# Both masks and both diagonals of a unit in one slot each, the second expert product two column tiles behind, and the first step's weight splits, states and chunks in the order of the first block's needs

## The chip, the cores and the metric

The kernel runs on one core of one Trainium2 chip. The time is device microseconds (us) of one execution. A kernel has one figure, the median of several runs. One execution is also taken by the profiler, and the rows in this document come from it.

Five queues run side by side, each in its own order: TensorE (PE, with its weight loads as PEld), VectorE (DVE), ScalarE (ACT), GpSimd (POOL) and the queue that issues transfers (SP). An instruction starts when the one ahead of it in its queue lets it and when the semaphores that it waits for are set.

## The reference

The computation is a linear attention with decay, followed by two gated expert layers. The sizes are: batch 4, 8 heads, 768 positions, head width 48.

```python
for t in range(S):                       # S = 768
    cur = np.einsum('bhd,bhe->bhde', u[None] * kt, vt)
    y[:, :, t] = np.einsum('bhd,bhde->bhe', rt, state + cur)
    state = w[None, :, :, None] * state + np.einsum('bhd,bhe->bhde', kt, vt)
x = y.transpose(0, 2, 1, 3).reshape(B * S, H * D)        # 3072 x 384
m = ((x @ w_a) * (x @ w_b)) @ w_out                      # width 1536
return (((m @ w1) * (m @ w2)) @ w3) @ w_out2             # width 1024
```

## The kernel before, in words

**Attention in chunks.** The 768 positions are cut into 6 chunks of 128. A chunk of one batch element is a unit, numbered 0 to 23 with the batch element running fastest, so units 0 to 3 are chunk 0 and units 4 to 7 chunk 1. A unit makes scores on PE (L363), takes the part below the diagonal with a mask on DVE (`a_evac`, L374, one instruction for each half of the heads), writes the diagonal into it (`a_diag`, L380, again one for each half), multiplies by the values (`y_mm`: L399 with the state, then L403 with the scores), and updates the state (`s_mm` L464, `s_decay` L471, `s_upd` L481). `prep_r`, `prep_k` and `prep_d` prepare the next unit's inputs, mostly on POOL; `k_nat` scales k there (L356). Units 0 to 3 have their own code ahead of everything else, because they have no state yet.

**Expert products.** A step is one chunk of all four batch elements, 512 columns. For each of 12 column tiles f, `ab_slots` makes two products on PE (two blocks of nine matmuls, L616). ACT copies the first to `g` (L635), DVE multiplies (L641), ACT rounds the product to `gh` (L642) and DVE makes the remainder `gl` (L647). `m_mm` then multiplies `gh` and `gl` by w_out in nine matmuls (L667 to L669) into three accumulators. Each operand is a high and a low part, which is why there are three matmuls for each product.

**Weight splits.** The weights arrive as 8-byte words. Class `Stream` turns each piece of 128x512 (a job) into a high and a low part: three DVE instructions convert the bits (L96, L112, L115, where L96 is that of the next job), ACT rounds the high part (`cast`, L128, followed by two range tests L131 and L150), and DVE subtracts to get the low part (L148). The first layer has 27 jobs: three for each of six groups of w_a and w_b columns (`wab0` to `wab5`, each used by two column tiles), and three for each of three groups of w_out rows (`wo0` to `wo2`, each used by four column tiles).

**What sets the order.** The order of the program text is the order in every queue; there is no scheduler. `merge` puts it together for each step: the main slots (products and `m_mm`), with the slots of the next chunk's units spread between them, and in the first step the remaining splits (`late`: `step` finishes a job and converts the next, `st.cast` rounds it) spread between these. A product's slot forces the splits that it needs. The prologue (the loop over u at L580) makes some splits itself: the tables `STEPS_U`, `STEPS_K` and `TAIL` say how many.

Of the kernel before, what the change touches and what calls it, by code (L numbers as in the profile page):

```python
# [7 lines left out]
F32 = mybir.dt.float32  # L8
# [12 lines left out]
C = 128  # L21
# [16 lines left out]

WARM, WARM_0 = 10, 6


STEPS_U = (1, 0, 0, 0)
STEPS_K = (0, 1, 1, 1)
TAIL = (1, 2)

S_NOW = 2
PRE = 3

END_0 = 4
LATE = 3  # L50
# [115 lines left out]
def rwkv_moe_kernel(ctx, tc, rkT, nat, wu, wab, wout, w12, w3T, wo2, r_in, k_in, v_in, w_in, u_in, out):  # L166
# [7 lines left out]
    def flat(ap):  # L174
        return ap.rearrange("p a b -> p (a b)")

    with tc.manual_schedule():
# [41 lines left out]
        wt, ut = wt[:, 0], wt[:, 1]  # L219
        load_rk(0)  # L220
        load_nat(0)
        u_bc = const.tile([128, DM], F32, name="u_bc")

        chk = const.tile([128, N64, 2], F32, name="chk")
        small = const.tile([128, 1], F32, name="small")
# [16 lines left out]
            for k in range(KD):  # L242
                wab_ready[i] = st.add(wab[i, :, k, :], lambda k=k: dst(k))

        def add_wout(i):
            def dst(s):
                if i not in wo_t:
                    wo_t[i] = [wop.tile([128, 4, DM], F32R, tag=f"wo{p}{i}", name=f"wo{p}{i}") for p in "hl"]
                return [flat(t)[:, s] for t in wo_t[i]]

            for j in range(3):
                s = slice(j * 512, (j + 1) * 512)
                wo_ready[i] = st.add(flat(wout[i])[:, s], lambda s=s: dst(s))

        def add_w12(i):
            w12_t[i] = [w12p.tile([128, KD, 512], F32R, name=f"w12{p}{i}") for p in "hl"]
            for k in range(KD):
                w12_ready[i] = st.add(w12[i, :, k, :], lambda k=k: [t[:, k, :] for t in w12_t[i]])

        for i in range(6):  # L260
            add_wab(i)
            if i % 2 == 0:
                add_wout(i // 2)
        st.AHEAD = 1
        for u in range(1, B):
            load_rk(u)
# [5 lines left out]
        def later_loads(u):  # L272
# [7 lines left out]
            elif u == 3:  # L280
# [5 lines left out]
        nc.gpsimd.memset(ident, 0.0)  # L286
        nc.gpsimd.affine_select(out=ident, in_=ident, compare_op=ALU.not_equal, fill=1.0,
                                base=0, pattern=[[-1, 128]], channel_multiplier=1)
        mask = const.tile([128, 128], F32, name="mask")
# [30 lines left out]
        tr = const.tile([112, NP, C], F32, name="tr")  # L320
        nc.vector.tensor_copy(out=tr[:, :, HALF:], in_=pos[:, :, 0:HALF])
        nc.vector.reciprocal(out=tr[:, :, 0:HALF], in_=pos[:, :, 1:][:, :, ::-1])
        tk = const.tile([112, NP, C], F32, name="tk")
# [127 lines left out]
        def s_mm(u):  # L451
            c, b = divmod(u, B)
            v = v_of(u)
            nat_t.pop(u, None)
            if c == NC - 1:
                return
            ps = (ps_at.tile([112, NP, D], F32, name="at") if c else
                  ps_m.tile([112, NP, D], F32, tag=("m2", "m0")[u % 2], name="s_ps"))
            at_ps["s", u] = ps
# [33 lines left out]
        def unit_slots(u):  # L493
            n = u + 1
            nxt = n < NU
            pool = nc.gpsimd

            def after(f, *a):
                if nxt:
                    f(n, *a)  # L500

            return [
                lambda: (scores(u), after(prep_r, pool)),
                lambda: (a_evac(u, 0), after(prep_k, pool)),
                lambda: (a_evac(u, 1), a_diag(u, 0), k_nat(u)),
                lambda: a_diag(u, 1),

                lambda: (y_mm(u), s_mm(u)),
                lambda: (load_rk(u + 2), load_nat(u + 2), y_evac(u), (u + 1) % B == 0 and y_shuffle(u // B), s_decay(u),
                         after(prep_d, 0)),  # L510
                lambda: (s_upd(u), after(prep_d, 1)),
                lambda: after(prep_d, 2),
            ]

# [46 lines left out]
            a_evac(u, 0)  # L561
            a_evac(u, 1)

        def steps(n):
            for _ in range(n):
                step()
                st.cast()

        prep_0(0)
        warm_up(WARM_0)  # L570
        scores_0(0)
# [8 lines left out]
        for u in range(B):  # L580
            if u + 1 < B:
                scores_0(u + 1)
                scores_d(u + 1)
            y_0(u)
            if u + 2 < B:
                prep_0(u + 2)
            if u + 1 < B:
                both_a(u + 1)
                diag_0(u + 1)
            y_0_evac(u)  # L590
            steps(STEPS_U[u])
            later_loads(u)
            if u == 2:
                tn_ps = ps_m.tile([128, NP, 112], F32, tag="m0", name="tn_ps")
                for p in range(NP):
                    mm(tn_ps[:, p, :], lhsT=tkw[:, p, :], rhs=ident[:112, :112], start=True, stop=True)
                tnat = const.tile([128, NP, 2, D], F32, name="tnat")
                for x, (a, e) in enumerate(XR):
                    nc.scalar.copy(out=tnat[:, :, x, :], in_=tn_ps[:, :, a:e])
            for b in ((), (), (0, 1), (2, 3))[u]:  # L600
                k_nat(b)
            steps(STEPS_K[u])
        steps(TAIL[0])
        for u in range(S_NOW):
            s_mm(u)
            s_upd(u)
        steps(TAIL[1])
        for f in prep_slots(B)[:PRE]:
            f()


        def ab_mm(ps, w, cs, x):
# [6 lines left out]
        def ab_slots(x, wget, keep):  # L619

            t = {}

            def run_a():
                w, ca, _ = wget()
                t["a"] = ps_ab.tile([128, TB], F32, name="ab")
                ab_mm(t["a"], w, ca, x())

            def run_b():
                w, _, cb = wget()
                t["b"] = ps_ab.tile([128, TB], F32, name="ab")  # L630
                ab_mm(t["b"], w, cb, x())

            def evac_a():
                t["g"] = gp.tile([128, TB], F32, tag="g", name="g")
                nc.scalar.copy(out=t["g"], in_=t["a"])  # L635

            def evac_b():
                g = t["g"]
                gh = gp.tile([128, TB], F32R, tag="gh", name="gh")
                gl = gp.tile([128, TB], F32R, tag="gl", name="gl")  # L640
# [16 lines left out]
        def m_mm(q, f):  # L657
            gh, gl = gt.pop((q, f))
            i, j = divmod(f, 4)
            if q == 0 and j == 0:  # L660
                st.split(wo_ready[i])
            if f == 0:
                m_ps[q] = [ps_m.tile([128, TB], F32, tag=f"m{k}", name=f"m{k}") for k in range(KD)]
            wh, wl = wo_t[i]
            for k in range(KD):
                cs = slice(k * 128, (k + 1) * 128)
                mm(m_ps[q][k], lhsT=wh[:, j, cs], rhs=gh, start=(f == 0), stop=False)  # L667
                mm(m_ps[q][k], lhsT=wh[:, j, cs], rhs=gl, start=False, stop=False)  # L668
                mm(m_ps[q][k], lhsT=wl[:, j, cs], rhs=gh, start=False, stop=(f == NF1 - 1))  # L669

        def m_evac(q):
            for k in range(KD):
                t = gp.tile([128, TB], F32, tag=("g", "gh", "gl")[k], name="m_sb")
                nc.scalar.copy(out=t, in_=m_ps[q][k])
                nc.sync.dma_start(out=m_d[q][:, k, :], in_=t)

# [46 lines left out]
        for q in range(NB):  # L723
            main = []
            for f in range(NF1):
                main += ab_slots(lambda q=q: xt[q], lambda q=q, f=f: w1_get(q, f),
                                 lambda *t, q=q, f=f: gt.__setitem__((q, f), t))
                lag.append((q, f))
                if len(lag) > 1:
                    main.append(m_slot(*lag.pop(0)))  # L730
            side = step_slots(q + 1)
            if q == 0:
                side = [lambda u=u: (s_mm(u), s_upd(u)) for u in range(S_NOW, B)] + prep_slots(B)[PRE:] + side
            if q == 0:
                late = [step, st.cast] * (len(st.jobs) - st.begun + 1)
                late += [lambda: None] * (len(late) // LATE)
# [359 lines left out]
```

## Time and profile before

| | |
|---|---|
| median of 3 runs | 926.12 us (925.85 to 927.89) |
| the profiled execution's own time | 927.42 us |
| its span, first to last instruction | 925.7 us |
| PE busy | 888.2 us, 96% |
| DVE busy | 447.2 us, 48% |
| ACT busy | 327.7 us, 35% |
| mean granted TensorE clock | 0.981 |

The span and the profiled execution's own time are of the same execution; 1.7 us lie outside the span. Busy shares are means over the whole span, and the kernel has stages with very different limits: the first 150 us and the rest have to be read apart.

### The profile page before, as it was taken

How to read it: one execution, taken by the hardware profiler on the slowest of the kernel's cores; microseconds unless marked ns; L12 is line 12 of the kernel's file. 1: busy time of each engine (PE TensorE's matmuls, PEld its weight loads, DVE VectorE, ACT ScalarE, POOL GpSimd, SP SyncE). 2: the span in 40 equal slices, each digit the busy share in tenths (PEclk: the TensorE clock that was granted, in tenths of full speed). 3: DMA queues.
4: the chain of work that ended last, by engine and by line, in shares of the span. 5: the costliest groups of instructions: out<-in, count | busy, mean ns of one | idle time of the engine just before them, and what ended most of it. 6: DMA issues, size and time to landing. Idle time of an engine off the chain costs nothing.

```text
span 925.7 us, 12522 instructions
## 1 busy us (share of the span) xinstructions
PE 888.2 (96%) x4962; PEld 753.1 (81%) x4962; DVE 447.2 (48%) x745; ACT 327.7 (35%) x737; POOL 122.0 (13%) x118
## 2 busy tenths in 40 slices
PE   8488879999999999999999999999999999999997
PEld 7366668888888888888888888899988888888886
DVE  8889894444334433443333789676332323222212
ACT  4375563322222223222121687655322212122211
POOL 2512322222222312320300000000000000000000
PEclk9789989999999999999999999999999999999999
DMA  8545432211222212222103345442020201010001
GB/s 250 180 142 170 145 114 63 80 46 59 65 66 64 78 47 71 66 64 64 62 2 106 127 146 189 143 146 95 12 69 0 69 1 57 12 35 1 35 0 38
DMA packets 26066, 73.57 MB, mean 79 GB/s; under 512 B 3152, under 2 KB 7376, under 8 KB 26000
## 3 DMA queue, kind: packets, MB, share of 16 engines
q1 hardware_dynamic: 26000, 72.70, 25.2%
q8 instruction: 41, 0.67, 0.3%
q14 instruction: 25, 0.20, 0.1%
HBM read 61.28 MB, written 9.44 MB: 76 GB/s over the span
## 4 chain that ended last, share of the span: by engine, by line
PE 86%; DVE 8%; ACT 2%; DMA 2%; issue 2%; SPq 0%; ACTq 0%
PE ab L616 50%; PE m L667 5%; PE m L668 5%; PE m L669 5%; PE at L764 4%; PE o L788 3%; PE o L789 3%; PE o L787 3%; PE at L403 2%; PE at L363 2%; DVE cvt L112 2%; DVE cvt L115 2%; PE at L399 2%; DVE cvt L96 1%; DMA rk<-in_rkT_dram 1%
## 5 line engine op out<-in xcount | busy, mean ns | idle before, releaser
L641 DVE TENSOR_TENSOR ab<-g,ab 128x512 f32<-128x512 f32 x120 | 83.4, 695 | 301.2 <-PE ab L616 299.8
L616 PE MATMUL ab<-xt,w12h 128*128 128x512 f32 x576 | 177.4, 389 | 0.0
L635 ACT COPY g<-ab 128x512 f32<-128x512 f32 x120 | 70.0, 583 | 250.5 <-PE ab L616 250.5
L642 ACT CAST gh<-ab 128x512 fp32r<-128x512 f32 x120 | 70.3, 586 | 239.4 <-DVE ab L641 239.4
L616 PEld LDWEIGHTS ab<-xt,w12h 128*128 128x128 f32 x576 | 107.5, 188 | 18.8
L647 DVE TENSOR_TENSOR gl<-ab,gh 128x512 fp32r<-128x512 f32 x120 | 82.8, 690 | 65.7 <-ACT gh L642 65.5
L616 PE MATMUL ab<-xt,w12l 128*128 128x512 f32 x288 | 112.0, 389 | 0.0
L668 PE MATMUL m<-gl,woh 128*128 128x512 f32 x216 | 84.9, 393 | 1.5 <-DVE gl L647 1.5
L667 PE MATMUL m<-gh,woh 128*128 128x512 f32 x216 | 86.2, 399 | 0.0
L669 PE MATMUL m<-gh,wol 128*128 128x512 f32 x216 | 84.5, 391 | 0.0
L336 POOL TENSOR_TENSOR rk<-rk,tr 112x512 f32<-112x512 f32 x20 | 27.4, 1368 | 293.1 <-DMA rk<-in_rkT_dram 249.0
L616 PEld LDWEIGHTS ab<-xt,w12l 128*128 128x128 f32 x288 | 54.1, 188 | 11.3
L616 PE MATMUL ab<-xt,wab0h 128*128 128x512 f32 x144 | 48.5, 420 | 4.2 <-ACT xt L427 4.2
L668 PEld LDWEIGHTS m<-gl,woh 128*128 128x128 f32 x216 | 40.8, 189 | 11.1 <-DVE gl L647 2.7
L667 PEld LDWEIGHTS m<-gh,woh 128*128 128x128 f32 x216 | 40.8, 189 | 9.9 <-issue 0.4
L669 PEld LDWEIGHTS m<-gh,wol 128*128 128x128 f32 x216 | 40.7, 188 | 8.6
L115 DVE SCALAR_TENSOR_TENSOR cvt<-stg_t,cvt 128x512 int32<-128x512 int32 x61 | 47.0, 770 | 0.3
L112 DVE SCALAR_TENSOR_TENSOR cvt<-stg_t,cvt 128x512 int32<-128x512 int32 x61 | 46.9, 770 | 0.3
L616 PE MATMUL ab<-xt,wab1h 128*128 128x512 f32 x144 | 46.6, 405 | 0.0
L616 PE MATMUL ab<-xt,wab2h 128*128 128x512 f32 x144 | 45.9, 400 | 0.0
L616 PE MATMUL ab<-xt,wab3h 128*128 128x512 f32 x144 | 45.4, 396 | 0.0
L616 PE MATMUL ab<-xt,wab4h 128*128 128x512 f32 x144 | 45.3, 396 | 0.0
(271 smaller groups left out, 1579.6 us busy)
## 6 DMA issues: line engine op xcount, KB each, us to landing
natt<-in_nat_dram SPq DMA_DIRECT2D x20, 576.0 KB, 5.0
rk<-in_rkT_dram SPq DMA_DIRECT2D x24, 448.0 KB, 3.8
stg_t<-in_wab_dram SPq DMA_DIRECT2D x18, 512.0 KB, 3.7
stg_t<-in_w3T_dram SPq DMA_DIRECT2D x16, 512.0 KB, 3.6
stg_t<-in_w_dram SPq DMA_DIRECT2D x12, 512.0 KB, 3.7
stg_t<-in_wout_dram SPq DMA_DIRECT2D x9, 512.0 KB, 3.8
m_d<-m_sb SPq DMA_DIRECT2D x18, 256.0 KB, 2.2
stg_t<-m_d SPq DMA_DIRECT2D x18, 256.0 KB, 2.6
```

The lines of the kernel that those rows point to most:

```text
L112: nc.vector.scalar_tensor_tensor(out=f, in0=w[:, :, 1], scalar=-0x40000000, in1=f, op0=ALU.bitwise_and, op1=ALU.bitwise_or)
L115: nc.vector.scalar_tensor_tensor(out=f, in0=w[:, :, 0], scalar=29, in1=f, op0=ALU.logical_shift_right, op1=ALU.bitwise_or)
L616: mm(ps, lhsT=w[i][:, k, cs], rhs=x[:, j, k, :], start=(n == 0), stop=(n == 3 * KD - 1))
L635: nc.scalar.copy(out=t["g"], in_=t["a"])
L641: nc.vector.tensor_tensor(out=t["b"], in0=g, in1=t["b"], op=ALU.mult)
L642: nc.scalar.copy(out=gh, in_=t["b"])
L647: nc.vector.tensor_tensor(out=gl, in0=t["b"], in1=gh, op=ALU.subtract)
L667: mm(m_ps[q][k], lhsT=wh[:, j, cs], rhs=gh, start=(f == 0), stop=False)
L668: mm(m_ps[q][k], lhsT=wh[:, j, cs], rhs=gl, start=False, stop=False)
L669: mm(m_ps[q][k], lhsT=wl[:, j, cs], rhs=gh, start=False, stop=(f == NF1 - 1))
L764: mm(f_ps[i], lhsT=w3_t[i][a][:, g, :], rhs=wo2_t[g // 4][b][:, g % 4, :], start=(n == 0), stop=(n == 3 * NF2 - 1))
L787: mm(o_ps[q][b], lhsT=ph[:, cs], rhs=wh, start=(f == 0), stop=False)
```

## The change

It has six parts, all in the order of the program text.

- A unit's two masks come in one slot, its two diagonals in the next, and `prep_d` part 0 moves into the slot that has become free.
- `m_mm` follows its column tile by two tiles in place of one; `gh` and `gl` have three buffers in place of two.
- The jobs of `wo` are no longer three in a row: the first of a group stands after an even `wab` group, the other two after the odd one; `m_mm` forces only the job that it needs.
- The prologue makes four steps in place of seven, one for each of its units; the cast of a job is issued one turn after its conversion.
- The four `k_nat`, the states of units 0 to 3 and the whole preparation of unit 4 are side slots of the first step; these states are made in the `ps_at` accumulators, where they were in two of the `m` accumulators.
- Some constants move to the pool that is released before the last layer.

```diff
-STEPS_U = (1, 0, 0, 0)
-STEPS_K = (0, 1, 1, 1)
-TAIL = (1, 2)
-S_NOW = 2
-PRE = 3
+STEPS = (1, 1, 1, 1)
...
         for i in range(6):
             add_wab(i)
-            if i % 2 == 0:
-                add_wout(i // 2)
+            add_wout(i // 2, ((0,), (1, 2))[i % 2])
...
-                lambda: (a_evac(u, 0), after(prep_k, pool)),
-                lambda: (a_evac(u, 1), a_diag(u, 0), k_nat(u)),
-                lambda: a_diag(u, 1),
+                lambda: (a_evac(u, 0), a_evac(u, 1), after(prep_k, pool)),
+                lambda: (a_diag(u, 0), a_diag(u, 1), k_nat(u)),
+                lambda: after(prep_d, 0),
...
             y_0_evac(u)
-            steps(STEPS_U[u])
+
+            st.cast()
+            for _ in range(STEPS[u]):
+                step()
             later_loads(u)
...
-            for b in ((), (), (0, 1), (2, 3))[u]:
-                k_nat(b)
-            steps(STEPS_K[u])
-        steps(TAIL[0])
-        for u in range(S_NOW):
-            s_mm(u)
-            s_upd(u)
-        steps(TAIL[1])
-        for f in prep_slots(B)[:PRE]:
-            f()
...
+                gh = gp.tile([128, TB], F32R, tag="gh", name="gh", bufs=3)
+                gl = gp.tile([128, TB], F32R, tag="gl", name="gl", bufs=3)
...
-            if q == 0 and j == 0:
-                st.split(wo_ready[i])
+            if q == 0:
+                st.split(wo_ready[i, min(j, 2)])
...
-                if len(lag) > 1:
+                if len(lag) > 2:
                     main.append(m_slot(*lag.pop(0)))
             side = step_slots(q + 1)
             if q == 0:
-                side = [lambda u=u: (s_mm(u), s_upd(u)) for u in range(S_NOW, B)] + prep_slots(B)[PRE:] + side
+                side = ([lambda u=u: k_nat(u) for u in range(B)] + [lambda u=u: (s_mm(u), s_upd(u)) for u in range(B)] +
+                        prep_slots(B) + side)
```

**ACT, end of the prologue.** `xt<-at` is the copy of a unit's attention output, `wab0h` the high part of a job, `sq` its range tests. Before, the last unit's copy stands behind the cast of job 2:

```order
13 L599 COPY tnat<-tn_ps 128x4x48 x2
14 L150 ACTIVATE sq,chk<-sq,small 128x512
15 L128 CAST wab0h<-cvt 128x512
16 L131 ACTIVATE sq,chk<-stg_t 128x512
17 L427 CAST xt<-at 128x3x128
```

Now it stands ahead of that cast, and the cast is followed by the first product's copy:

```order
14 L589 COPY tnat<-tn_ps 128x4x48 x2
15 L421 CAST xt<-at 128x3x128
16 L122 CAST wab0h<-cvt 128x512
17 L125 ACTIVATE sq,chk<-stg_t 128x512
18 L144 ACTIVATE sq,chk<-sq,small 128x512
19 L615 COPY g<-ab 128x512
```

What moved is the copy of unit 3 (two rows up, past the cast), and the casts of jobs 3 to 6, which are now behind the first products' copies.

**DVE, unit 5.** Before, its masks (`a_sc<-at,mask`) and diagonals (`a_sc<-ident,dg`) lie one by one among the splits:

```order
115 L374 TENSOR_TENSOR a_sc<-at,mask 128x512
116 L148 TENSOR_TENSOR wab3l<-cvt,wab3h 128x512
117 L112 SCALAR_TENSOR_TENSOR cvt<-stg_t,cvt 128x512
118 L96 TENSOR_SCALAR cvt<-stg_t 128x512
119 L115 SCALAR_TENSOR_TENSOR cvt<-stg_t,cvt 128x512
120 L374 TENSOR_TENSOR a_sc<-at,mask 128x512
121 L380 COPY_PREDICATED a_sc<-ident,dg 128x512
122 L641 TENSOR_TENSOR ab<-g,ab 128x512
123 L647 TENSOR_TENSOR gl<-ab,gh 128x512
124 L380 COPY_PREDICATED a_sc<-ident,dg 128x512
```

Now they stand in pairs:

```order
119 L368 TENSOR_TENSOR a_sc<-at,mask 128x512 x2
120 L621 TENSOR_TENSOR ab<-g,ab 128x512
121 L142 TENSOR_TENSOR wol_745<-cvt,woh_744 128x512
122 L106 SCALAR_TENSOR_TENSOR cvt<-stg_t,cvt 128x512
123 L90 TENSOR_SCALAR cvt<-stg_t 128x512
124 L109 SCALAR_TENSOR_TENSOR cvt<-stg_t,cvt 128x512
125 L627 TENSOR_TENSOR gl<-ab,gh 128x512
126 L374 COPY_PREDICATED a_sc<-ident,dg 128x512 x2
```

Between the first mask and the last diagonal there is one split and one column tile's pair (`ab`, `gl`) either way; ahead of the last diagonal stand 17 low parts (L148, now L142) and six `gl` now, 16 and five before.

**PE, up to unit 7's `y_mm`.** Before, the last rows ahead of it are the ninth `m_mm`:

```order
241 L616 MATMUL ab<-xt,wab4h 128x512 x2
242 L616 MATMUL ab<-xt,wab4l 128x512
243 L667 MATMUL m_635<-gh,woh_1077 128x512
244 L668 MATMUL m_635<-gl,woh_1077 128x512
245 L669 MATMUL m_635<-gh,wol_1078 128x512
```

Now they are the eighth, with w_out rows of the group ahead (`woh_744`):

```order
232 L596 MATMUL ab<-xt,wab4h 128x512 x2
233 L596 MATMUL ab<-xt,wab4l 128x512
234 L647 MATMUL m_639<-gh,woh_744 128x512
235 L648 MATMUL m_639<-gl,woh_744 128x512
236 L649 MATMUL m_639<-gh,wol_745 128x512
```

In both, 20 product blocks (column tiles 0 to 9) and the scores of units 4 to 7 are ahead of unit 7's `y_mm`; one `m_mm` has moved behind it.

## Rows read from the trace of the kernel before

**Rows 1.** The page: busy time of PE and PEld, share, instructions.

```profile
PE 888.2 (96%) x4962; PEld 753.1 (81%) x4962; DVE 447.2 (48%) x745; ACT 327.7 (35%) x737; POOL 122.0 (13%) x118
```

**Rows 2.** Windows: stretch, length, busy of the five engines, granted clock, DMA share, GB/s.

```profile
40.00:50.00 10.00, 3.35 (x22) 2.81 (x23) 7.67 (x13) 7.24 (x19) 1.25 (x2) 0.50 0.33 107
120.00:130.00 10.00, 7.85 (x50) 6.80 (x51) 8.78 (x18) 7.43 (x20) 1.55 (x2) 0.68 0.65 205
200.00:250.00 50.00, 50.00 (x299) 41.15 (x299) 18.72 (x32) 11.29 (x26) 11.09 (x10) 1.00 0.18 51
```

**Rows 3.** Waits of PE, whole span: total us, times, longest.

```profile
PE at L403 <- DVE a_sc L380: 12.1, 5, 3.2
PE s_ps L464 <- issue: 7.0, 1, 7.0
PE ab L616 <- ACT xt L427: 4.2, 1, 4.2
PE m L668 <- DVE gl L647: 1.5, 3, 0.8
```

**Rows 4.** Timeline of PE, 120 to 145 us: start, length, instruction, idle before.

```profile
122.15 1.73 PE L403 MATMUL at<-a_sc,natt 128*48 128x128 f32 x13 [2.16 <-DVE a_sc L380]
...
135.06 0.62 PE L616 MATMUL ab<-xt,wab4h 128*128 128x512 f32 x2
...
139.18 0.39 PE L667 MATMUL m<-gh,woh 128*128 128x512 f32 x1
...
141.22 1.04 PE L399 MATMUL at<-rk,s 112*112 112x128 f32 x8
142.19 1.08 PE L403 MATMUL at<-a_sc,natt 128*48 128x128 f32 x16
```

**Rows 5.** DVE by line, 35.7 to 142 us: count, busy, mean ns, idle before.

```profile
L115 DVE SCALAR_TENSOR_TENSOR cvt<-stg_t,cvt 128x512 int32<-128x512 int32 x24 | 20.8, 865 | 0.0
L96 DVE TENSOR_SCALAR cvt<-stg_t 128x512 int32<-128x512 int32 x23 | 14.7, 638 | 0.0
L148 DVE TENSOR_TENSOR wol<-cvt,woh 128x512 fp32r<-128x512 f32 x9 | 6.3, 695 | 3.7 <-ACT woh L128 3.5
L441 DVE TENSOR_TENSOR y<-at,y 112x128 fp32r<-112x128 f32 x3 | 0.9, 284 | 1.9 <-ACT xt L440 1.9
```

**Rows 6.** Timeline of DVE, 35 to 46 us.

```profile
35.30 0.56 DVE L428 TENSOR_TENSOR xt<-at,xt 128x384 fp32r<-128x384 f32 x1 [1.71 <-ACT xt L427]
35.77 1.53 DVE L148 TENSOR_TENSOR wab0l<-cvt,wab0h 128x512 fp32r<-128x512 f32 x1
...
42.49 0.69 DVE L148 TENSOR_TENSOR wol<-cvt,woh 128x512 fp32r<-128x512 f32 x1 [0.68 <-ACT woh L128]
43.10 0.68 DVE L112 SCALAR_TENSOR_TENSOR cvt<-stg_t,cvt 128x512 int32<-128x512 int32 x1
43.70 0.42 DVE L96 TENSOR_SCALAR cvt<-stg_t 128x512 int32<-128x512 int32 x1
44.03 0.68 DVE L115 SCALAR_TENSOR_TENSOR cvt<-stg_t,cvt 128x512 int32<-128x512 int32 x1
45.40 0.69 DVE L148 TENSOR_TENSOR wol<-cvt,woh 128x512 fp32r<-128x512 f32 x1 [0.68 <-ACT woh L128]
```

**Rows 7.** Timeline of DVE, 70 to 73 us: a multiply ahead of a low part.

```profile
70.37 0.69 DVE L641 TENSOR_TENSOR ab<-g,ab 128x512 f32<-128x512 f32 x1
72.23 0.69 DVE L148 TENSOR_TENSOR wab2l<-cvt,wab2h 128x512 fp32r<-128x512 f32 x1 [1.17 <-ACT wab2h L128]
```

**Rows 8.** Timeline of POOL, 28 to 42 us.

```profile
28.11 4.94 POOL L356 TENSOR_TENSOR k<-k,tnat 128x384 f32<-128x384 f32 x4 [8.37 <-ACT tnat L599]
...
40.08 1.17 POOL L356 TENSOR_TENSOR kn<-natt,tnat 128x384 f32<-128x384 f32 x1
```

**Rows 9.** Timeline of DVE: the last diagonals of units 6 and 7.

```profile
121.37 0.72 DVE L380 COPY_PREDICATED a_sc<-ident,dg 128x512 f32<-128x512 int32 x1
...
140.57 1.36 DVE L380 COPY_PREDICATED a_sc<-ident,dg 128x512 f32<-128x512 int32 x2
```

More of the change, by code (lines that the diff above doesn't have):

```diff
@@ L221, in rwkv_moe_kernel @@
         load_nat(0)
-        u_bc = const.tile([128, DM], F32, name="u_bc")
+        u_bc = att.tile([128, DM], F32, name="u_bc", bufs=1)
         chk = const.tile([128, N64, 2], F32, name="chk")
@@ L243, in add_wab, with add_wout @@
                 wab_ready[i] = st.add(wab[i, :, k, :], lambda k=k: dst(k))
-        def add_wout(i):
+        def add_wout(i, part):
             def dst(s):
@@ L249, in dst @@
                 return [flat(t)[:, s] for t in wo_t[i]]
-            for j in range(3):
+            for j in part:
                 s = slice(j * 512, (j + 1) * 512)
-                wo_ready[i] = st.add(flat(wout[i])[:, s], lambda s=s: dst(s))
+                wo_ready[i, j] = st.add(flat(wout[i])[:, s], lambda s=s: dst(s))
         def add_w12(i):
@@ L288, in rwkv_moe_kernel @@
                                 base=0, pattern=[[-1, 128]], channel_multiplier=1)
-        mask = const.tile([128, 128], F32, name="mask")
+        mask = att.tile([128, 128], F32, name="mask", bufs=1)
         nc.gpsimd.memset(mask, 1.0)
@@ L319, in rwkv_moe_kernel @@
                 initial=1.0, op0=ALU.mult, op1=ALU.add)
-        tr = const.tile([112, NP, C], F32, name="tr")
+        tr = att.tile([112, NP, C], F32, name="tr", bufs=1)
         nc.vector.tensor_copy(out=tr[:, :, HALF:], in_=pos[:, :, 0:HALF])
         nc.vector.reciprocal(out=tr[:, :, 0:HALF], in_=pos[:, :, 1:][:, :, ::-1])
-        tk = const.tile([112, NP, C], F32, name="tk")
+        tk = att.tile([112, NP, C], F32, name="tk", bufs=1)
         nc.vector.tensor_copy(out=tk, in_=tr[:, :, ::-1])
@@ L456, in s_mm @@
                 return
-            ps = (ps_at.tile([112, NP, D], F32, name="at") if c else
-                  ps_m.tile([112, NP, D], F32, tag=("m2", "m0")[u % 2], name="s_ps"))
-            at_ps["s", u] = ps
+            ps = at_ps["s", u] = ps_at.tile([112, NP, D], F32, name="at")
             kn = kn_t.pop(u)
@@ L503, in unit_slots @@
                 lambda: (scores(u), after(prep_r, pool)),
-                lambda: (a_evac(u, 0), after(prep_k, pool)),
-                lambda: (a_evac(u, 1), a_diag(u, 0), k_nat(u)),
-                lambda: a_diag(u, 1),
+                lambda: (a_evac(u, 0), a_evac(u, 1), after(prep_k, pool)),
+                lambda: (a_diag(u, 0), a_diag(u, 1), k_nat(u)),
+                lambda: after(prep_d, 0),
                 lambda: (y_mm(u), s_mm(u)),
                 lambda: (load_rk(u + 2), load_nat(u + 2), y_evac(u), (u + 1) % B == 0 and y_shuffle(u // B), s_decay(u),
-                         after(prep_d, 0)),
-                lambda: (s_upd(u), after(prep_d, 1)),
+                         after(prep_d, 1)),
+                lambda: s_upd(u),
                 lambda: after(prep_d, 2),
@@ L562, in both_a @@
             a_evac(u, 1)
[L564 to L567, printed above, removed]
         prep_0(0)
@@ L596, in rwkv_moe_kernel @@
                     mm(tn_ps[:, p, :], lhsT=tkw[:, p, :], rhs=ident[:112, :112], start=True, stop=True)
-                tnat = const.tile([128, NP, 2, D], F32, name="tnat")
+                tnat = att.tile([128, NP, 2, D], F32, name="tnat", bufs=1)
                 for x, (a, e) in enumerate(XR):
                     nc.scalar.copy(out=tnat[:, :, x, :], in_=tn_ps[:, :, a:e])
-            for b in ((), (), (0, 1), (2, 3))[u]:
-                k_nat(b)
-            steps(STEPS_K[u])
-        steps(TAIL[0])
-        for u in range(S_NOW):
-            s_mm(u)
-            s_upd(u)
-        steps(TAIL[1])
-        for f in prep_slots(B)[:PRE]:
-            f()
         def ab_mm(ps, w, cs, x):
@@ L638, in evac_b @@
                 g = t["g"]
-                gh = gp.tile([128, TB], F32R, tag="gh", name="gh")
-                gl = gp.tile([128, TB], F32R, tag="gl", name="gl")
+                gh = gp.tile([128, TB], F32R, tag="gh", name="gh", bufs=3)
+                gl = gp.tile([128, TB], F32R, tag="gl", name="gl", bufs=3)
                 nc.vector.tensor_tensor(out=t["b"], in0=g, in1=t["b"], op=ALU.mult)
@@ L672, in m_evac @@
             for k in range(KD):
-                t = gp.tile([128, TB], F32, tag=("g", "gh", "gl")[k], name="m_sb")
+                t = gp.tile([128, TB], F32, tag=("g", "gh", "gl")[k], name="m_sb", bufs=(2, 3, 3)[k])
                 nc.scalar.copy(out=t, in_=m_ps[q][k])
```

## The prediction

> **What bounds the kernel now.** The page first: PE is busy 888.2 of 925.7 us [rows 1], so all that can be won on PE without removing work is some 37 us, plus what a lower clock costs. The windows come next, to see where those 37 us lie. From 200 us on PE is busy in all of a stretch, at full clock [rows 2], and this holds for the rest but the tail. The loss is ahead of 130 us: between 40 and 50 us PE is busy 3.35 us of ten at a granted clock of 0.50, its 1.2 GHz level, and between 120 and 130 us 7.85 of ten at 0.68 [rows 2]. The list of waits, third, names what PE waits for: 12.1 us in five waits for a diagonal (L380) ahead of `y_mm`; 7.0 us once for the accumulators of `s_mm`, with no releaser shown; 4.2 us for unit 3's output copy; only 1.5 us for `gl` ahead of `m_mm` [rows 3]. Last, the timeline of the engine that releases them: DVE, which from 36 to 142 us has almost no gap. In 106.2 us (from the low part of job 2 at 35.77 to the end of unit 7's diagonals, 140.57 + 1.36) it does 24 whole splits and everything else that the first step needs [rows 6, 9]. So the bound of this stretch is the DVE queue, and PE's waits are the places where PE catches up with it. PE's last such wait ends at 122.15; at unit 7's `y_mm`, at 142.19, it has no wait and never has one again in this step [rows 4].
>
> This gives the way to count. In both kernels PE runs without a gap behind unit 7's `y_mm`. What the change is worth is when PE gets there, and how much of PE's work is then still ahead of it.
>
> **The work ahead of that point.** Counted in the DVE queue of both kernels, from job 2's low part to unit 7's last diagonal there stand the same instructions: 25 low parts, 24 conversions, nine multiplies and nine `gl`, eight masks, eight diagonals. The order differs, the sum does not. On PE both have 20 product blocks and the scores of units 4 to 7 there, but eight `m_mm` in place of nine.
>
> **Start of the DVE chain.** Before, unit 3's copy on ACT stands behind job 2's cast, and DVE waits 1.71 us for it ahead of L428 [rows 6]. Now the copy is done early. What is late next is the cast of job 2 itself, which starts when its conversion ends and takes about the 0.68 us that DVE waits at 42.49, while L428 runs [rows 6]. So the chain starts at 34.3 in place of 35.77: minus 1.5 us.
>
> **The four `k_nat`.** They leave the prologue's text, but the queue of POOL is the same, row for row, so they run where they ran: from 28.11, when `tnat` is there, with the rest of POOL's chain to 41.25 [rows 8]. `tnat` comes a little later, behind two range tests. DVE instructions are slowed by POOL: a low part takes 1.53 us at 35.77 and 0.69 at 42.49, when POOL is done [rows 6]. Nothing is won here.
>
> **What POOL costs DVE in all.** L115 has a mean of 0.865 us and 0.68 when undisturbed, 24 times: 4.4 us. L112 has the same count and mean. L96 has 0.638 against 0.42, 23 times: 5.0 us [rows 5, 6]. With the slow low parts that is 15 us. After, POOL's work falls elsewhere: the second unit's sums fall on a multiply, a `gl` and masks, whose input lies in an accumulator; the rest falls on conversions again. I take minus 2.5 us, with bounds of minus 5 (a third of it goes) and plus 3.
>
> The Trainium skill ("SBUF — State Buffer", section "Who interferes with whom") says that a VectorE instruction with two SBUF inputs contends with a GpSimd instruction that reads SBUF, and one with at most one SBUF input, outside the two-port modes, does not. The slow low part agrees with it. By it the diagonals, whose inputs are both in SBUF, can be caught too; no row here shows one so.
>
> **DVE's idle time.** The lines of DVE have 10.4 us of idle time in this stretch, the `wol` row with 3.7 the largest and the wait for `y`, 1.9, the next [rows 5]. There are two kinds. A low part straight behind its conversion waits for the cast: 0.68 us [rows 6]. A low part straight behind a multiply, where ACT has `gh` ahead of the cast, waits 1.17 [rows 7]. In the new queues I find four of the first (about as many as before) and five of the second where there were three: plus 2.4. Jobs 7 and 8 are cast behind the copies of the first four states and of the products, which now come in between: 1.3 us each, less 0.5 saved at jobs 4 and 5: plus 2.1. Sum plus 4.5 us. Bounds: 0, since ACT itself is not full, and 9, each wait twice as long.
>
> **The time of unit 7's `y_mm`.** By the DVE chain its diagonals end at 141.93 - 1.5 - 2.5 + 4.5 = 142.4. By PE's own path: unit 6's last diagonal ended at 122.1 [rows 9]; now one split (0.61 + 0.60 + 0.33 + 0.60 = 2.14 us [rows 6]) and one column tile's pair (1.2) more stand ahead of it, so with the start (-1.5), most of the idle time (+3.7) and of POOL's (-1.4) it ends at 126.1. From PE's release there to unit 7's `y_mm` were 20.04 us (122.15 to 142.19), with four product blocks and three `m_mm` [rows 4]. Now there are three and two. An `m_mm` takes 2.04 us (139.18 to 141.22), a block 2.06 (135.06 to 139.18 is two) [rows 4]: 15.9 us, and PE is there at 142.0. The later of the two counts, though the first heads need only the first diagonal: 142.3, against 142.19. PE comes out of its prologue early, and loses that lead again in a long wait, some 10 us, for unit 6's diagonals.
>
> **What is left behind it.** One `m_mm` more: plus 2.04 us. The two-tile distance itself is worth at most the 1.5 us that PE waits for `gl` [rows 3], which lie in the DVE-bound stretch and are in the count. The 7.0 us wait for `s_mm` and the 4.2 us [rows 3] go too, for the same end: PE is earlier, DVE is not. Pairs of diagonals give `y_mm` one slot more of distance; what is late then is the pair itself, behind 23 splits. Later steps have no split, DVE is 37% busy there (18.72 of 50) and PE has no wait [rows 2], so the moved slots, the third `gh` and `gl` buffers and the moved constants cost nothing; without this cover a late pair of masks would cost PE one, 1.2 us.
>
> **Sum.** 142.3 - 142.19 + 2.04 = plus 2.1 us. The profiled execution took 927.42 us, so 929.5; the median of the runs shown is 1.3 us lower, so 928.2. A measurement of this kernel can tell about 0.2%, 1.85 us, from no change, so this is just at its edge.
>
> **Rivals.**
>
> Faster: ACT does not hold DVE more than before. The place is jobs 4 to 8, where casts stand behind `gh` and the copies of states. For it: ACT is busy 35% [rows 1]. Against it: the order, in which the cast is behind `gh`, and `gh` behind the DVE multiply. Without the 4.5 us PE gets to unit 7's `y_mm` at 138 and the time is 926.1 - 2.2 = 923.9. It decides from where unit 6's diagonals end ahead of 124.2 (142.19 - 2.04 - 15.9).
>
> Much faster: the order keeps PE fed, and the waits (12.1 + 7.0 + 4.2 + 1.5 [rows 3]) and the low clock go: 926.1 - 24.8 = 901 us, or less. For it: each wait named is taken up by a part of the change. Against it: the equal DVE content; DVE would have to lose 25 us out of 106, and only its 10 us of idle and 15 of POOL are not work.
>
> Slower still: a pair of diagonals, or a run of conversions, is caught by POOL. A caught instruction takes 0.8 us more [rows 6]; a pair in three units and a job or two make 4 us: 932. It decides where POOL's window (some 4 to 7 us a unit) falls just ahead of `y_mm`.
>
> **How the numbers follow.** The forecast has a chance of 0.56, the faster rival 0.25, the much faster one 0.05, the slower one 0.14. The forecast spreads from 926 to 931 with its bounds for idle time and POOL: 0.03 of it faster, 0.26 same, 0.27 slower. The faster rival lies across the edge: 0.16 faster, 0.09 same. So: faster 0.24, same 0.35, slower 0.41. The range from 922.5 to 932.5 leaves out the much faster rival, the ends of the idle bounds, and half of the slower rival.
>
> **What would show it.** Right: DVE's first split after the prologue at about 34.3; no wait of 7 us at `s_mm`; product blocks one behind the other from 34; waits of PE for the diagonals of units 5 and 6, the second about 10 us; unit 6's diagonals ending near 126; unit 7's `y_mm` near 142 with eight `m_mm` done. Wrong: unit 6's diagonals ending ahead of 124, or PE idle for weights (L616 waiting for a low part) in place of diagonals by more than a few us.

## The result and the profile after

The changed kernel takes **931.38 us** (median of 5 runs, 931.17 to 932.36), 1.0058 of before (95% interval 1.0046 to 1.0069): slower by 5.3 us, where 2.1 were forecast. The profiled execution took 931.78 us, its span is 930.0 us, 4.3 more than before's 925.7. The other 0.9 of the 5.3 is no difference of the two traces: before's profiled execution lay 1.3 us above its median, this one 0.4.

The page's busy line, which answers to [rows 1]:

```profile
PE 895.4 (96%) x4962; PEld 757.7 (81%) x4962; DVE 446.6 (48%) x745; ACT 329.6 (35%) x737; POOL 122.1 (13%) x118
```

The instructions are the same. PE's idle time is 2.9 us less in sum (34.6 for 37.5) and its busy time 7.2 more, at a mean granted clock of 0.977 for 0.981, so what was won in waits was spent in slower matmuls. The windows, which answer to [rows 2]:

```profile
40.00:50.00 10.00, 3.29 (x6) 1.62 (x6) 8.60 (x12) 5.76 (x15) 3.90 (x3) 0.71 0.51 166
120.00:130.00 10.00, 5.20 (x45) 4.03 (x43) 8.24 (x15) 5.66 (x13) 0.57 (x1) 0.81 0.32 99
200.00:250.00 50.00, 50.00 (x299) 40.93 (x297) 18.70 (x32) 11.25 (x26) 11.88 (x11) 1.00 0.19 51
```

PE is as starved as before between 40 and 50 us, more so between 120 and 130, and full from 200 us on. The difference lies ahead of that again. PE's waits, total, times and longest, against [rows 3]:

```profile
PE at L397 <- DVE a_sc L374: 8.7, 4, 4.7
PE ab L596 <- ACT g L615: 4.6, 1, 4.6
PE ab L596 <- ACT wab1h L122: 3.4, 2, 2.4
PE at L357 <- DVE s L473: 3.0, 1, 3.0
PE ab L596 <- ACT wab2h L122: 2.1, 1, 2.1
...
PE ab L596 <- DVE wab2l L142: 1.3, 1, 1.3
PE ab L596 <- ACT xt L421: 0.8, 1, 0.8
```

The four waits that the change aims at are gone or smaller (12.1 to 8.7, 7.0 and 1.5 to none, 4.2 to 0.8), 15.3 us in all. In their place stand waits for a product's copy, for weights and for scores' accumulators: 4.6 + 3.4 + 3.0 + 2.1 + 1.3 = 14.4 us. They moved; they did not go. PE's timeline at the last of them and at unit 7's `y_mm`, against [rows 4]:

```profile
126.77 2.34 PE L397 MATMUL at<-a_sc,natt 128*48 128x128 f32 x15 [4.72 <-DVE a_sc L374]
...
143.01 1.04 PE L393 MATMUL at<-rk,s 112*112 112x128 f32 x8
144.34 0.42 PE L397 MATMUL at<-a_sc,natt 128*48 128x128 f32 x2 [0.29 <-DVE a_sc L374]
```

Unit 7's `y_mm` starts at 144.34 for 142.19, 2.15 later, with one `m_mm` (2.04) more behind it: 4.2, and the span is 4.3 longer. So the whole loss lies ahead of this point and in that one `m_mm`.

DVE by line from 30.9 to 145 us (the same stretch of its queue as [rows 5]):

```profile
L106 DVE SCALAR_TENSOR_TENSOR cvt<-stg_t,cvt 128x512 int32<-128x512 int32 x24 | 22.3, 931 | 0.0
L109 DVE SCALAR_TENSOR_TENSOR cvt<-stg_t,cvt 128x512 int32<-128x512 int32 x24 | 18.8, 784 | 0.0
L90 DVE TENSOR_SCALAR cvt<-stg_t 128x512 int32<-128x512 int32 x23 | 12.3, 536 | 0.0
L142 DVE TENSOR_TENSOR wol<-cvt,woh 128x512 fp32r<-128x512 f32 x9 | 7.2, 804 | 5.5 <-ACT woh L122 5.5
```

and single instructions of it, from DVE's timeline:

```profile
30.93 0.72 DVE L142 TENSOR_TENSOR wab0l<-cvt,wab0h 128x512 fp32r<-128x512 f32 x1
31.58 1.50 DVE L106 SCALAR_TENSOR_TENSOR cvt<-stg_t,cvt 128x512 int32<-128x512 int32 x1
...
56.05 0.69 DVE L142 TENSOR_TENSOR wol<-cvt,woh 128x512 fp32r<-128x512 f32 x1 [2.20 <-ACT woh L122]
...
125.99 1.34 DVE L374 COPY_PREDICATED a_sc<-ident,dg 128x512 f32<-128x512 int32 x2
...
130.13 2.37 DVE L142 TENSOR_TENSOR wab5l<-cvt,wab5h 128x512 fp32r<-128x512 f32 x1 [0.69 <-ACT wab5h L122]
...
141.65 1.28 DVE L368 TENSOR_TENSOR a_sc<-at,mask 128x512 f32<-128x512 f32 x2
142.85 2.04 DVE L374 COPY_PREDICATED a_sc<-ident,dg 128x512 f32<-128x512 int32 x2
```

beside POOL's:

```profile
30.01 5.11 POOL L350 TENSOR_TENSOR k<-k,tnat 128x384 f32<-128x384 f32 x4 [11.40 <-ACT tnat L589]
...
129.43 1.28 POOL L330 TENSOR_TENSOR rk<-rk,tr 112x512 f32<-112x512 f32 x1 [10.76 <-PE at L397]
130.66 1.28 POOL L334 TENSOR_TENSOR rk<-rk,tk 112x512 f32<-112x512 f32 x1
131.90 1.46 POOL L350 TENSOR_TENSOR kn<-natt,tnat 128x384 f32<-128x384 f32 x1
141.21 1.41 POOL L339 TENSOR_TENSOR pr<-natt,u_bc 128x384 f32<-128x384 f32 x1 [7.85 <-DVE dg L344]
142.70 1.00 POOL L341 TENSOR_TENSOR pr<-pr,natt 128x384 f32<-128x384 f32 x1
```

Three figures of the DVE chain are read from the timeline for every kernel below: its **start** (job 2's low part, 35.77 before, 30.93 after), its **idle** time up to the end of unit 7's diagonals (9.7 and 15.4; gaps under 0.15 us are not counted), and what POOL costs it, the **excess** of conversions, low parts and diagonals over their undisturbed 0.42, 0.68, 0.69 and 0.72 us (15.2 and 17.2). The end of unit 7's diagonals went from 141.93 to 144.89: -4.8 + 5.7 + 2.0 = +2.9.

The start is not a matter of the order alone. In this trace PE's granted clock is 0.52 from 20 to 27 us, which is its 1.2 GHz level in nearly all of the stretch. Before it is 1.00 there, and it is 1.00 in two kernels below whose prologue is the same (one tile of distance, and `step` and cast in one slot). PE was busy 8.1 of the 10 us ahead of it in the changed kernel and in the one with one tile alike. The changed kernel's window:

```profile
20.00:27.00 7.00, 6.88 (x57) 6.09 (x56) 7.00 (x13) 0.67 (x3) 0.00 (x0) 0.52 0.29 88
```

and, of the kernel with one tile of distance, the same window and lines of POOL's and DVE's timelines:

```profile
20.00:27.00 7.00, 5.39 (x66) 4.50 (x68) 7.00 (x13) 3.23 (x10) 0.00 (x0) 1.00 0.34 91
27.01 4.94 POOL L350 TENSOR_TENSOR k<-k,tnat 128x384 f32<-128x384 f32 x4 [8.82 <-ACT tnat L589]
33.19 1.39 DVE L142 TENSOR_TENSOR wab0l<-cvt,wab0h 128x512 fp32r<-128x512 f32 x1 [0.22 <-ACT wab0h L122]
```

At the low clock PE's product for `tnat` (L586) starts at 26.86, at the full clock at 23.77; so POOL's run starts at 30.01 and lets job 2's conversion pass ahead of it, or at 27.01 and catches it, and the chain starts at 30.93 or at 33.19. What the early start wins goes back to POOL in part: the excess is 17.2 here, 16.6 in the kernel with the slots of before, whose POOL starts at 29.68, and 14.3 and 15.4 in the two at full clock. Start and excess together bring the end forward by 2.8 us here and by 2.0 to 3.8 in the other three.

### The profile page after: what moved, and what is told of

Read it like the earlier page. It is cut to its first block, busy times and chain, and to the rows that moved or that the text cites. A ratio compares the mean times of both kernels' runs of the same rounds, so it can differ in the third digit from the quotient of the medians.

```text
span 930.0 us, 12516 instructions
## 1 busy us (share of the span) xinstructions
PE 895.4 (96%) x4962; PEld 757.7 (81%) x4962; DVE 446.6 (48%) x745; ACT 329.6 (35%) x737; POOL 122.1 (13%) x118
## 4 chain that ended last, share of the span: by engine, by line
PE 85%; DVE 9%; issue 3%; ACT 2%; DMA 1%; SPq 0%; DVEq 0%; ACTq 0%
PE ab L596 49%; PE m L647 5%; PE m L648 5%; PE m L649 5%; PE at L745 4%; PE o L769 3%; PE o L768 3%; PE o L770 3%; DVE cvt L106 2%; PE at L357 2%; PE at L397 2%; DVE cvt L109 2%; PE at L393 2%; DVE cvt L90 1%; DMA rk<-in_rkT_dram 1%
## 5 line engine op out<-in xcount | busy, mean ns | idle before, releaser
L106 DVE SCALAR_TENSOR_TENSOR cvt<-stg_t,cvt 128x512 int32<-128x512 int32 x61 | 47.7, 782 | 0.3
L596 PE MATMUL ab<-xt,wab0h 128*128 128x512 f32 x144 | 45.7, 398 | 0.9 <-ACT xt L421 0.8
L596 PE MATMUL ab<-xt,wab5h 128*128 128x512 f32 x144 | 45.0, 394 | 0.0
```

The lines of the kernel that those rows point to most:

```text
L106: nc.vector.scalar_tensor_tensor(out=f, in0=w[:, :, 1], scalar=-0x40000000, in1=f, op0=ALU.bitwise_and, op1=ALU.bitwise_or)
L596: mm(ps, lhsT=w[i][:, k, cs], rhs=x[:, j, k, :], start=(n == 0), stop=(n == 3 * KD - 1))
```

## The experiments

Theory: DVE's queue bounds the first 145 us, and the time is the start of unit 7's `y_mm` plus a constant, less 2.04 us for each `m_mm` done by then. Rivals: PE's own waits for weights and accumulators set the time, or one part of the change (the pairs, the distance) is a loss by itself. Most runs of one kernel lie within 1.5 us of their median, a few up to 2.7 away.

**Is DVE the bound?** One of the three conversions is left out of the changed kernel:

```diff
-            nc.vector.scalar_tensor_tensor(out=f, in0=w[:, :, 1], scalar=-0x40000000, in1=f,
-                                           op0=ALU.bitwise_and, op1=ALU.bitwise_or)
```

> The changed kernel without the second of the three conversion instructions of a split (the sign bit of the weights is left out). Theory (the vector queue is the bound until unit 7): 24 instructions of 0.6 us, and up to 0.8 us more where GpSimd slows them, leave the chain, unit 7's diagonals end 15 to 18 us earlier and the time falls by 10 to 16 us: 915 to 921 us. Rival (TensorE's own order or ScalarE is the bound, and the vector queue is only busy): 929 to 931 us.

Measured: 916.1 us (0.9892 of before, 0.9877 to 0.9907). The diagonals of unit 7 end at 128.87, 16.0 earlier than in the changed kernel, and the time is 15.3 lower. That is in the range of the theory. DVE is the bound, and its end passes through to the time nearly whole.

**What do POOL's reads cost?** Its products up to unit 8 become writes (the same for `tk`, `pr` and `kn`), so that their part of the computation is left out:

```diff
-            eng.tensor_tensor(out=r, in0=r, in1=flat(tr), op=ALU.mult)
+            if eng is nc.gpsimd and u <= 8:
+                eng.memset(r, 0.0)
```

> The changed kernel in which GpSimd's products up to unit 8 (scaling of r and k, the diagonal's products, the scaled k) are replaced by constants written to the same tiles, so GpSimd reads nothing there; its part of the computation is left out. Theory (GpSimd's reads slow the vector instructions with two inputs in SBUF by some 15 us in the first step, and this is on the bound): no slowed conversions, unit 7's diagonals end some 10 us or more earlier, 917 to 924 us. Rival (the slowing hides in the waits for ScalarE's casts, or writes slow as much as reads): 929 to 931 us.

Measured: 914.95 us (0.9879, 0.9864 to 0.9895), 16.4 less than the changed kernel. DVE by line, 30 to 128 us, and one of POOL's writes:

```profile
L109 DVE SCALAR_TENSOR_TENSOR cvt<-stg_t,cvt 128x512 int32<-128x512 int32 x24 | 16.5, 687 | 0.0
L106 DVE SCALAR_TENSOR_TENSOR cvt<-stg_t,cvt 128x512 int32<-128x512 int32 x24 | 16.5, 686 | 0.0
L90 DVE TENSOR_SCALAR cvt<-stg_t 128x512 int32<-128x512 int32 x23 | 9.9, 428 | 0.0
```

```profile
32.78 0.53 POOL L331 MEMSET rk<- 112x512 f32 x1 [9.83 <-DMA rk<-in_rkT_dram]
```

The conversions are back at 0.69 and 0.43 us, the excess falls from 17.2 to 0.15, and the idle time stays (16.0). Without POOL's reads the time is 16 us lower, 2 more than the theory gave, and its writes cost DVE 0.15. These 16 us hold POOL's shorter instructions too; the next experiment keeps the work.

**The work of POOL given to DVE.** In the kernel before, the preparations of units 4 to 8 and the first eight `k_nat` go to DVE, some five instructions of 0.54 to 0.68 us a unit:

```diff
         def prep_k(u, eng):
+            if u <= 8:
+                eng = nc.vector
```

> The kernel before with the preparation of units 4 to 8 and the scaled k of units 0 to 7 on the vector engine in place of GpSimd. Theory (GpSimd costs the vector chain some 15 us in the first step, more than the work itself costs there): the work adds some 12 us to the chain (0.46 to 0.6 us each), the slowing of 15 us goes, so 2 to 4 us less: 922 to 924 us. Rival (the added work counts in full and the slowing mostly hid in waits for ScalarE): 930 us or more.

Measured: **920.84 us** (0.9943, 0.993 to 0.9957), better than both kernels and 1.2 below the range of the theory. The bound engine got more work and finished it earlier: unit 7's diagonals end at 136.72 for 141.93. DVE by line, 35.7 to 137 us:

```profile
L112 DVE SCALAR_TENSOR_TENSOR cvt<-stg_t,cvt 128x512 int32<-128x512 int32 x24 | 16.4, 683 | 0.0
L338 DVE TENSOR_TENSOR rk<-rk,tr 112x512 f32<-112x512 f32 x5 | 3.4, 682 | 0.0
```

**One tile of distance.** The changed kernel with `m_mm` one tile behind again:

```diff
-                if len(lag) > 2:
+                if len(lag) > 1:
```

> The changed kernel with the second expert product one column tile behind, as before. Theory (the vector queue sets when unit 7's y_mm may start, and the two-tile distance leaves one product more behind that point): unit 7's diagonals end where they do in the changed kernel, 144.9 us, with nine products done in place of eight, so 2.0 us less: 929.3 us. Rival (the distance itself costs nothing, the loss is all in the vector queue): 931.4 us, the same as the changed kernel.

Measured: 927.68 us (1.0021, 1.0011 to 1.0031), 3.7 less than the changed kernel, and less than either expectation. Of that 2.04 is the `m_mm`; for the other 1.7 the trace has unit 7's diagonals at 142.94 for 144.89. Part of this goes with the prologue's clock: the chain starts 2.3 later (33.19) and has 2.9 less excess (14.3), 0.6 together. The rest is 1.4 less idle time (14.0). And with POOL's preparations on DVE, one tile first, then two:

> The changed kernel with the second product one tile behind and with the same preparations on the vector engine. Theory: 927.7 us of the one-tile kernel less the same 2 to 4 us: 923.5 to 925.7 us. Rival: 931 us or more.

> The changed kernel, two column tiles behind, with the same work moved from POOL to DVE; against the run with the one-tile distance (920.86 us). Theory: the second tile of distance leaves one m_mm of 2.04 us more behind unit 7's y_mm, and nothing in the first step pays for it: 922.4 to 923.4 us, y_mm at 134 to 135 with eight m_mm done. Rival: with POOL away the looser distance lets PE go on where it waits for gl, and costs nothing: 920.4 to 921.4 us.

Measured: 920.86 us (0.9946, 0.9933 to 0.996), 2.6 below the range expected, and 924.51 us (0.9986, 0.9977 to 0.9995), 1.1 above it: some 3.6 for the second tile, nearly twice one `m_mm`. DVE idles 11.4 and 13.3 us, and unit 7's diagonals end at 135.01 and 136.53. With two tiles one wait is longer, that of DVE's timeline at 49.90:

```profile
49.90 0.69 DVE L142 TENSOR_TENSOR wol<-cvt,woh 128x512 fp32r<-128x512 f32 x1 [1.85 <-ACT woh L122]
```

which is 0.51 with one. So the distance costs some 3.6 us in either setting: 2.04 as foreseen, and some 1.5 in a later DVE chain, which was not. In both settings the chain shows it as idle time, 1.4 and 1.8 us. The changed order with one tile and POOL's preparations on DVE (920.86) is as fast as the order of before with the same move (920.84), so with one tile the changed order wins nothing over it.

**The early start.** In the kernel before, each cast of the prologue is issued one turn later:

```diff
-                step()
                 st.cast()
+                step()
```

> The kernel before with one edit: in the prologue a job is cast one turn after its conversion, so unit 3's copy on ScalarE is ahead of job 2's cast, as in the changed kernel. Theory (the early start of the vector chain is a gain of its own, in part taken back since GpSimd's products then fall on more of the chain): job 2's low part at 31 to 34 us in place of 35.8, unit 7's diagonals 1 to 3 us earlier, 923 to 925.5 us. Rival (the start is worth nothing, GpSimd takes all of it back): 926 us, no change.

Measured: 927.19 us (1.0013, 1.0004 to 1.0022): the rival was right, there is no gain. The chain starts 2.2 earlier (33.53), and POOL, still in its prologue's run, catches the conversions that now come under it (DVE's timeline):

```profile
33.53 1.00 DVE L148 TENSOR_TENSOR wab0l<-cvt,wab0h 128x512 fp32r<-128x512 f32 x1 [0.22 <-ACT wab0h L128]
34.45 1.49 DVE L112 SCALAR_TENSOR_TENSOR cvt<-stg_t,cvt 128x512 int32<-128x512 int32 x1
35.86 1.23 DVE L96 TENSOR_SCALAR cvt<-stg_t 128x512 int32<-128x512 int32 x1
37.01 1.75 DVE L115 SCALAR_TENSOR_TENSOR cvt<-stg_t,cvt 128x512 int32<-128x512 int32 x1
```

In this one trace the chain still ends 1.9 earlier (140.04), and the profiled execution, 926.61, is 0.8 below before's; the medians don't show it. PE keeps the lead to its end: DVE's last copy of the output (`o_sb`, L796) starts at 917.23 for 919.03. The other 1.0 is lost behind that copy, where the span has 7.7 us for 6.7. With POOL out of the way:

> The kernel before with POOL's preparations of units 4 to 8 and the first eight k_nat on DVE (920.84 us measured), and each cast of the prologue issued one turn later, ahead of the step. Theory: an early start of the DVE chain was no gain in the kernel before (927.19 us) because POOL's reads, which stay where they are, then catch more of the conversions; with POOL away from that stretch the start 2.4 us earlier passes through: 918.2 to 919.2 us, unit 7's diagonals end near 134.4. Rival: the cast is late for the jobs behind it, whatever POOL does, and the earlier start is given back as idle time of DVE: 920.5 to 921.2 us.

Measured: **919.24 us** (0.9923, 0.9909 to 0.9937), 1.6 below the kernel without the later cast; the two intervals overlap a little. The chain starts 2.6 earlier and ends 2.4 earlier. This speaks for the theory: a start counts when POOL's reads don't take it back. It is the fastest of the kernels that leave nothing out.

**The pairs.** The unit's slots of before in the changed kernel:

```diff
-                lambda: (a_evac(u, 0), a_evac(u, 1), after(prep_k, pool)),
-                lambda: (a_diag(u, 0), a_diag(u, 1), k_nat(u)),
-                lambda: after(prep_d, 0),
+                lambda: (a_evac(u, 0), after(prep_k, pool)),
+                lambda: (a_evac(u, 1), a_diag(u, 0), k_nat(u)),
+                lambda: a_diag(u, 1),
```

> The changed kernel with the masks, diagonals and sums of a unit in the slots of before, one by one. Theory (the vector queue counts, not the pairing): one remainder more (1.2 us with its multiply) stands ahead of unit 7's last diagonal, so 931 to 933 us. Rival (the pairs hold the queue up and are the loss): 926 to 928 us.

Measured: 933.74 us (1.0077, 1.0063 to 1.0091). The pairs are worth 2.4 us in the changed kernel, so they are not the loss. The same edit at one tile's distance, with POOL's preparations on DVE:

> The changed kernel with the one-tile distance and POOL's preparations on DVE (920.86 us measured), and each unit's masks and diagonals in slots of their own again, as before the change. Undone in the changed kernel, the pairs cost 2.4 us more; added to the kernel before they cost 3.4 us, so their sign depends on the order around them. If it is the order of jobs and of the prologue that makes pairs pay: 922.8 to 923.8 us. If it is the two-tile distance, which is gone here: 917 to 919 us. In both, the span less the start of unit 7's y_mm stays near 783.5 us with nine m_mm done.

Measured: 928.01 us (1.0022, 1.0014 to 1.0031), 7.2 more than with pairs; both expectations missed the size, and the second the sign. PE's timeline:

```profile
137.03 0.42 PE L402 MATMUL at<-a_sc,natt 128*48 128x128 f32 x2 [0.71 <-DVE a_sc L379]
140.05 1.73 PE L402 MATMUL at<-a_sc,natt 128*48 128x128 f32 x13 [2.60 <-DVE a_sc L379]
```

and its window from 140 to 200 us, and that of the kernel with pairs:

```profile
140.00:200.00 60.00, 59.95 (x366) 49.42 (x366) 22.79 (x40) 15.85 (x37) 16.51 (x15) 0.96 0.22 65
```

```profile
140.00:200.00 60.00, 60.00 (x353) 49.21 (x352) 24.02 (x41) 14.49 (x32) 14.59 (x14) 1.00 0.20 55
```

The second diagonal stands behind one more column tile's pair, and `y_mm` waits for it in its midst: 5.0 us later (140.05 for 135.07). Behind the wait of 2.60 the granted clock has a mean of 0.96 over 60 us, where it is 1.00 without: 2.4 us more. The sum is 7.4. Last, pairs in the kernel before (with POOL's preparations on DVE and the later cast):

> The kernel before with POOL's preparations on DVE, the later cast, and both masks and both diagonals of a unit in one slot each. Theory: pairs save 2.4 us here as they did in the changed kernel (undone there: plus 2.4): 1.5 to 2.5 us below the same kernel without pairs, 916 to 918 us. Rival: with the one-tile distance the pair stands one split earlier ahead of the same y_mm, DVE's work ahead of unit 7's diagonals is unchanged, and the time is that of the kernel without pairs within 0.7 us.

Measured: 922.6 us (0.9955, 0.994 to 0.997), 3.4 more than without pairs: neither theory nor rival. Unit 7's diagonals end earlier (133.69 for 134.33), but PE reaches its `y_mm` at 137.06 for 134.87, since it waits at the scores now:

```profile
97.37 0.46 PE L368 MATMUL at<-rk 48*128 48x128 f32 x2 [1.62 <-issue]
...
122.43 0.46 PE L368 MATMUL at<-rk 48*128 48x128 f32 x2 [2.98 <-issue]
```

No such wait is in the kernel without pairs. The trace names no releaser; that the scores wait for accumulators that the unit's state still holds is likely from the row behind it (another 0.68 for DVE's `s`), and not shown. So the worth of pairs hangs on the order around them: +2.4, +7.2, -3.4.

**Can DVE's idle time be had?** In the changed kernel, `step` and the cast go into one slot, so that a cast is ahead of `gh`:

```diff
-                late = [step, st.cast] * (len(st.jobs) - st.begun + 1)
+                late = [lambda: (step(), st.cast())] * (len(st.jobs) - st.begun + 1)
```

> The changed kernel with a step and the cast of its job always in one piece, so that a cast no longer comes behind the rounding of a product on ScalarE. Theory (the vector queue's idle time behind multiplies, five times 1.17 us, is on the bound): idle time of the vector chain falls from 15 to about 10 us and the time by 3 to 5 us: 926.5 to 928.5 us. Rival (the waits only move to another place of the chain): 930.5 to 932 us.

Measured: 931.99 us (1.0063, 1.005 to 1.0077). The waits of 1.17 behind a multiply fall to one, and DVE waits for PE in their place:

```profile
58.69 0.70 DVE L621 TENSOR_TENSOR ab<-g,ab 128x512 f32<-128x512 f32 x1 [4.09 <-PE ab L596]
```

while PE waits 5.5 us (3.4 in the changed kernel) for `wab1h`. The idle sum is 15.2 for 15.4: the rival was right.

**The account over all of them.** Span less start of unit 7's `y_mm` is 783.2 to 784.7 us in the seven kernels with nine `m_mm` done and no wait of 2 us at it, 785.7 to 785.8 in the four with eight. The step between them is the `m_mm`'s 2.04; the highest of the seven, 784.7, is the later cast with its longer end. In the three others PE waits 2 us or more in or just ahead of that `y_mm`, and they lie 2 to 5 us above.

## Why the prediction came near, and what it had wrong

**The bound and the way to count** held: DVE sets unit 7's diagonals, PE has no wait behind them, and one `m_mm` more is left behind. All three were shown. The measured time lies in the range, but its terms did not come out one by one: the start was 3.3 us better than forecast, POOL's share 4.5 worse and the idle time 1.2 worse, which is the 2.4 us that unit 7's diagonals came later than the 142.4 forecast. That misses cancel is in part the mechanism, since start and POOL's share hang together, and in part luck. (By its own terms the count for unit 6's diagonals gives 126.2 and not 126.1; nothing else changes by it.)

**PE's path** from its release at unit 6's diagonals to unit 7's `y_mm` (L403, now L397) was 15.9 and measured 17.6 (126.77 to 144.34), with the three blocks and two `m_mm` that were counted. Of the difference 0.3 is a wait, and 1.2 is clock. The window of this path, and that of the path of before that the 15.9 was worked out from:

```profile
126.77:144.34 17.57, 17.27 (x101) 13.97 (x102) 15.63 (x24) 10.21 (x27) 6.34 (x5) 0.82 0.19 61
122.15:142.19 20.04, 20.04 (x117) 16.64 (x117) 18.76 (x30) 13.43 (x35) 6.46 (x5) 0.90 0.26 79
```

The granted clock is 0.82 for 0.90, and 0.18 of 17.57 less 0.10 of 20.04 is 1.2 us. The forecast took the clock of before. So PE's own count was 2 us short as well (142.0 forecast; 144.34 less the wait is 144.05), and the two counts still met. The four `k_nat` ran in one piece as before (5.11 us for 4.94); what their move is worth by itself no run shows.

**The start** was sized at -1.5 and came to -4.8 in this trace, -2.6 and -2.2 in the two of the same prologue at full clock. The prediction has the shift of `tnat` in the two range tests. They were not it: at full clock POOL's run starts at 27.01 and 27.43 with the same tests ahead, earlier than the 28.11 of before [rows 8]. PE's low clock between 20 and 27 us moved it to 30.01, so that job 2's conversion lay ahead of it, undisturbed. The prediction did not ask what such a shift uncovers, nor what the clock of the prologue would be.

**POOL's share** is the term that was farthest off: -2.5 forecast, +2.0 measured (15.2 to 17.2). The lead of the start goes back to POOL at once (1.50 at 31.58), and later low parts and a pair are caught: 2.37 at 130.13 beside POOL's `rk` and `kn`, 2.04 at 142.85 for 1.34. The rival "slower still" named this mechanism and 932 us, and the result lies nearer to it than to the forecast. Against it, the kernels that differ from the changed one in a line or a few (distance, slots, cast) have an excess of 14.3, 16.6 and 15.4, so a term of 2 us here is not a property of the change: it goes with the start, and both with the prologue's clock. Two terms that the prediction summed as independent are in part one. The two masks ahead of that pair took 1.28 us, undisturbed, beside POOL's product at 141.21, and the pair 2.04 beside the one at 142.70. The masks have one input in SBUF, the diagonals two. The Trainium skill ("SBUF — State Buffer", section "Who interferes with whom") has the first kind free of contention with GpSimd outside the two-port modes, and the second kind contend with a GpSimd instruction that reads SBUF, not with one that only writes it. These rows and the run with POOL's writes agree with that. The prediction had no row for a caught diagonal; this is one. The conversion L90 (L96 before) is caught too, with one input in SBUF (1.23 us at 35.86 in the run with the later cast, 0.42 undisturbed); whether it runs in a two-port mode no run shows.

**DVE's idle time**: +4.5 forecast, +5.7 measured. Five waits of 1.17 came as counted; the largest, 2.20 at 56.05, was not counted.

**The distance** was costed at one `m_mm` and nothing in the first step. It costs some 3.6 us, of the 5.3: the 1.5 or so beyond the `m_mm` are a later DVE chain. With one tile the change is at 1.0021.

**Where PE waits** was half wrong. Unit 6's diagonals ended at 127.33 (126.1 forecast), but PE lost its lead earlier, in 14.4 us of waits for a copy, weights and accumulators, and waited 4.7 there in place of 10. Of these, 6.8 us were for weights (3.4 + 2.1 + 1.3). By the prediction's own words that is a sign against it; the time did not mind, since PE's lead was to be lost in any case.

**Left open**: whether the longer end behind the last copy, seen in one trace, is why the later cast alone shows no gain in medians; what holds the scores in the kernel before with pairs; why PE's clock in the prologue was low in some traces and not in others of the same text. The order of the jobs, the prologue's four steps and the chunks as side slots were never changed one by one. Together they are no small thing: with POOL's preparations on DVE, one tile and no pairs in both, the changed order takes 928.01 us and the order of before, with the later cast, 919.24, and which of them costs what was not shown.

## What to carry to other kernels

Where one engine's queue bounds a stretch, count what stands ahead of its last product on both engines: waits that a new order removes elsewhere come back under other names, and only the content, the idle time of that queue and what is left behind count. Ask what else reads SBUF beside a bound VectorE: giving it GpSimd's work won 5 us here, while this reordering lost as much. A start that depends on another engine's clock is no fixed term, and what an early start wins must be counted together with what then falls under GpSimd's reads. Judge a slot's shape in the order it will run in, since the same pairing was worth 2 to 7 us in one and cost 3 in another.

## What was not expected of the hardware

Some 36 us of GpSimd's work (122.0 us less the 86.3 that stay when it is moved) cost VectorE 14 to 17 us; as writes they cost 0.15. A short wait cost more than itself here: behind 2.60 us of idle TensorE the mean granted clock of the next 60 us was 0.96, as 4.8 us at the 1.2 GHz level make it, which is 2.4 us lost. In the two other traces with a wait of 2 us or more there (the slots of before, and `step` with its cast) it was 0.97 from 140 to 200 us, where it was 1.00 without such a wait. And TensorE's clock in the prologue, 0.52 or 1.00, moved the start of VectorE's chain by 2.3 us, through the start of GpSimd's run. The same conversion of 0.68 us took 1.50, and a low part of 0.69 up to 2.37.
